# Four of sixteen weight preparation jobs of layer two placed, part by part, behind attention steps of eight later head pairs

## The chip, the cores and the metric

The kernel runs on one core of one Trainium2 chip. The metric is the device time of one execution in microseconds (us), the median of several runs. Matrix products run on TensorE (PE, with its weight loads as PEld), elementwise work on VectorE (DVE) and ScalarE (ACT), reductions over partitions on GpSimd (POOL); SyncE (SP) issues nearly all DMA transfers.

## The reference

Three stages follow one another. The first is attention with random features over 4 x 8 heads of 576 positions, head size 64, 128 features:

```python
proj = einsum('bhsd,df->bhsf', x, w_phi)
proj = proj - max(abs(proj), axis=-1, keepdims=True)
phi  = concatenate([exp(proj), exp(-proj)], axis=-1)
kv   = einsum('bhsf,bhsd->bhfd', phi(k), v);  z = sum(phi(k), axis=2)
out  = (phi(q) @ kv) / (phi(q) @ z + 1e-06)
```

Its output, as 2304 tokens of 512 values, goes through layer one, `max(0.01*h, h) @ w_out` with `h = x @ w_in` (512 to 2048 to 512), and then through layer two, `(h * sigmoid(h)) @ w_out`, with weights of its own of the same sizes. The weights of the layers come as 64-bit floats, so each must be turned into 32-bit ones on the chip.

## The kernel before

**Precision.** Each operand of the layers is held as a high part and a low part (`split`, L683: ACT copies the high part, DVE subtracts it, L262), and a product is three matmuls. Layer one takes the tokens in five tiles (`tiles1`: 462, 462, 460, 460, 460) and the hidden size in 16 chunks. For each (tile, chunk), `h_mm` (L821) does 12 matmuls (L830) into a bank of the set "a", `h_g` applies the leaky ReLU on ACT (tile g, L836), `h_high` and `h_low` split the result (gh on ACT, L841; gl on DVE), and `y_mm` (L851) does 12 matmuls (L861) of them with `wo[c]`, one chunk late. From the second tile on, `wo[c]` is loaded back from memory by `load_wo` (L783): 512 KB on SP, from the ring "wo1", and from the ring "wo2" once attention is over.

**Attention** runs in 16 pairs of heads. The first eight are done in an order written out by hand; the later eight (8 to 15) go one after the other between some 187 and 385 us, in the shadow of layer one, each over three chunks of a tile. The list `seq` holds their steps with a due time each, from the offsets in `OFF1` (L606): lv, lq (loads), sp (split), pq, pk, pkt (projections), eq0 and eq1 (exponentials of q, by halves), kv, num0 and num1 (numerators and denominators, L571 and L572 on ACT: tiles d and x), fin0 and fin1 (multiply x by the reciprocal of the denominator, and split it into the xh and xl of a token tile, L407). `run_att` (L630) takes the steps that are due from `seq` and writes them; the main loop calls it twice per (tile, chunk). The order on each engine is then made by a scheduler, which keeps data dependences and what `behind` asks for: `behind(spot, f, ...)` runs f and holds its instructions, on each engine, behind the one that `spot` names for that engine.

**Weight preparation of layer two** is `prep_w7` (L700), a generator of five parts per job, 2 x 8 jobs. Part one loads 512 KB of raw weights on SP (`load64`, ring "raw") and narrows them to fa: ACT takes the absolute value t (L657) and scales the other word to r (L658), DVE does four operations (L664, 665, 666, 670). Part two does the same for fb. Part three forms two pairs of sums on DVE (L717 to L720). Part four puts fa and half of fb: `put` splits into a tile wst (ACT L684, DVE L262) and SP stores it in `w7s` (L713). Part five puts the sums. `jobs_of` (L1060) gives each part a cost of 1.8, the last 1.6.

Before the change, `run_jobs` (L1075) takes parts only once `seq` is empty, with 3.4 credits for each of the remaining (tile, chunk) steps, so the first job begins near 360 us. What is left of the sixteen jobs after layer one is done in the first groups of layer two, up to a given job before each.

Of the kernel before, what the change touches and what calls it, by code (L numbers as in the profile page):

```python
# [9 lines left out]
F32R = mybir.dt.float32r  # L10
# [111 lines left out]
def tile_linear_attention_ffn_ffn(ctx: ExitStack, tc: tile.TileContext, q, k, v, w_phi, w_in1, w_out1, w_in2, w_out2, out):  # L122


    nc = tc.nc
# [9 lines left out]
    WOB = 3  # L135
    RAWB = 3
# [7 lines left out]
    wp = ctx.enter_context(tc.tile_pool(name="wp", bufs=1))  # L144
# [27 lines left out]
    pins = {mybir.EngineType.PE: [], mybir.EngineType.Activation: [], mybir.EngineType.DVE: [], mybir.EngineType.SP: []}  # L172

    def in_order(f, i, ts):

        seen = len(nc.cur_bb.bb.instructions)
        f(i)
        m, was = 0, None
        for ins in nc.cur_bb.bb.instructions[seen:]:
            if ins.engine in pins:  # L180
                m, was = min(m + (was not in (None, ins.engine)), len(ts) - 1), ins.engine
                pins[ins.engine].append((ts[m], ins))
# [11 lines left out]
    def behind(first, f, *a):  # L194

        seen = len(nc.cur_bb.bb.instructions)
        r = f(*a)
        nosync = mybir.DependencyInfo(mybir.DependencyClass.NoSync, mybir.DependencyReason.DATA)
        for ins in nc.cur_bb.bb.instructions[seen:]:
            if ins.engine in first:  # L200
                tc.add_manual_dep(ins, first[ins.engine].name, nosync, reason="order")
        return r
# [128 lines left out]
    def part(i, a):  # L331

        return ((0, 256), (256, 320))[a] if full(i) else ((0, HALF), (HALF, HALF))[a]
# [273 lines left out]
    seq = [(t, i, n_) for n_, ts in ORDER.items() for i, t in enumerate(ts)]  # L607
# [9 lines left out]
    seq.sort()  # L617
    seq.reverse()

    def missing(t):  # L620
        a0, n0 = tiles1[t]
        for _, i, n_ in seq:
            if n_[:3] in ("fin", "ffx"):
                c0, w = part(i, int(n_[3]))
                lo = i // HP * S + c0
                if lo < a0 + n0 and lo + w > a0:
                    return True
        return False

    def run_att(until, tile_=None):  # L630
        while seq and (seq[-1][0] < until or (tile_ is not None and missing(tile_))):
            if AB[0] is ABUFS0 and seq[-1][2] in OFF1:
                att0_ctx.close()
                att_pool[0] = att_ctx.enter_context(tc.tile_pool(name="att1", bufs=1))
                AB[0] = ABUFS1
            t, i, n_ = seq.pop()
            PRO[0] = t < RING
            if n_ in head or (i, n_) in EARLY:
                in_order({**fns, **head}[n_], i, EARLY.get((i, n_), (t,)))
            else:  # L640
                behind(low if n_[:3] == "fin" else {}, fns[n_], i)


    x2 = drp.tile([KD, 128, NT], F32, name="x2")
# [2 lines left out]
    def load64(src):  # L647

        raw = wp.tile([128, 512, 2], U32, tag="raw", bufs=RAWB, name="raw")
        nc.sync.dma_start(raw, src)  # L650
        return raw
# [27 lines left out]
    def narrow64(raw):  # L679

        return narrow_dve(*narrow_act(raw))

    def split(f, h, l):  # L683
        nc.scalar.activation(h, f, AF.Copy)  # L684
        sub(l, f, h)
# [8 lines left out]
    def words(w, c):  # L694
        return w.bitcast(U32)[c].rearrange("p (f t) -> p f t", t=2)

    def load_wo64(w, c):
        return load64(w.bitcast(U32)[c * 128 : (c + 1) * 128, :].rearrange("p (f t) -> p f t", t=2))

    def prep_w7(m_, p):  # L700

        ld = (lambda c: load64(words(w_in2, c))) if m_ == 0 else (lambda c: load_wo64(w_out2, c))
        fa = narrow64(ld(2 * p))
        yield
        fb = narrow64(ld(2 * p + 1))
        yield
        lo, hi = slice(0, 256), slice(256, 512)

        def put(i, x):
            m = x.shape[1] // 256  # L710
            o = wp.tile([128, m, 2, 256], F32R, tag="wo1", bufs=WOB, name="wst")
            split(x.rearrange("p (m f) -> p m f", f=256), o[:, :, 0], o[:, :, 1])
            nc.sync.dma_start(w7s[m_, p, :, i : i + m], o.bitcast(F32))  # L713

        s12 = wp.tile([128, 512], F32, tag="t64", bufs=2, name="s12")
        s34 = wp.tile([128, 512], F32, tag="t64", bufs=2, name="s34")
        nc.vector.tensor_tensor(s12[:, lo], fb[:, lo], fb[:, hi], op=ALU.add)  # L717
        nc.vector.tensor_tensor(s12[:, hi], s12[:, lo], fa[:, lo], op=ALU.subtract)
        nc.vector.tensor_tensor(s34[:, lo], fa[:, lo], fb[:, lo], op=ALU.subtract)
        nc.vector.tensor_tensor(s34[:, hi], fa[:, hi], s12[:, hi], op=ALU.subtract)  # L720
        yield
        put(0, fa)
        put(2, fb[:, hi])
        yield
        put(3, s12)
        put(5, s34)
# [328 lines left out]
    wake()  # L1055
    split_consts()
    run_att(END - 1e-3)
    pin()

    def jobs_of(m, p):  # L1060
        for _ in prep_w7(m, p):
            half[0] = True
            yield NP * m + p, 1.8
        half[0] = False
        yield NP * m + p, 1.6

    jobs = (x for m in range(2) for p in range(NP) for x in jobs_of(m, p))
# [14 lines left out]
    for s, (t, c) in enumerate((t, c) for t in range(len(tiles1)) for c in range(NC)):  # L1082
        if s < len(SLOTS):
            continue
        run_att(T0 + pace(s + 0.5) + 0.21, t if c == 0 else None)
        emit_h(t, c)
        run_att(T0 + pace(s + 1) + 0.21)
        if prev is not None:
            emit_y(*prev)
        prev = (t, c)  # L1090
        if not seq and s1p[0] is None:
            att_ctx.close()
            s1p[0] = ctx.enter_context(tc.tile_pool(name="s1", bufs=1))
        if s1p[0] is not None:
            run_jobs(RATE[0])
            if t == len(tiles1) - 1:
                if c in (2, 5):
                    settle()
                    next(x_first)
                if c >= 9:  # L1100
                    next(h_first)
# [103 lines left out]
```

## Time and profile before

| | us |
|---|---|
| median of 3 runs | 939.24 (939.15 to 939.47) |
| the profiled execution | 938.98 |
| its span, first to last instruction | 937.2 |
| PE busy | 931.2 (99%) |
| weight loads of PE busy | 882.5 (94%) |
| DVE busy | 646.3 (69%) |
| ACT busy | 598.2 (64%) |
| POOL busy | 77.7 (8%) |

A busy share is of the whole span. The profile divides the span into stages only where windows are asked for, and idle time of an engine is put down to what ended it. An engine's operations overlap a little at their ends, so two neighbours may show less time from start to start than the first one's length.

### The profile page before, as it was taken

To read this page: it belongs to the slowest core of one execution; us is meant where nothing else is said; L and a number is where in the kernel's file an instruction comes from. 1 tells how busy PE (TensorE), PEld (TensorE's weight loads), DVE (VectorE), ACT (ScalarE), POOL (GpSimd) and SP (SyncE) were. 2 spreads that over 40 slices of the span, in tenths; PEclk is the share of its full clock that TensorE was granted. 3 is DMA by queue.
4 is the path that set the end of the run, shared out by engine and by line. 5 is a ranking of instruction groups with operands and counts; after the bars stand their busy time and mean duration, and the time that the engine had idled before them with its cause. 6 is when DMAs were issued, how large, how long until landed. Compare 5 with 4: busy or idle time off the path is not lost.

```text
span 937.2 us, 15718 instructions
## 1 busy us (share of the span) xinstructions
PE 931.2 (99%) x5430; PEld 882.5 (94%) x5430; DVE 646.3 (69%) x1280; ACT 598.2 (64%) x1224; POOL 77.7 (8%) x50
## 2 busy tenths in 40 slices
PE   8999999999999999999999999999999999999998
PEld 7999989999999999988888999999999999999998
DVE  6889999966656655587777577879553685534853
ACT  6888787877777775565554456666644556444553
POOL 4442000111111110000000000000000000000000
PEclk9999999999999999999999999999999999999999
DMA  6854474573333434699999987998898778986785
GB/s 228 283 181 165 147 247 150 175 232 106 116 122 96 129 102 122 216 391 352 350 323 359 377 306 288 351 350 298 271 303 274 239 245 270 307 277 219 250 268 164
DMA packets 101759, 226.13 MB, mean 241 GB/s; under 512 B 15024, under 2 KB 25264, under 8 KB 101680
## 3 DMA queue, kind: packets, MB, share of 16 engines
q1 hardware_dynamic: 100432, 220.14, 69.2%
q0 software_dynamic: 960, 4.72, 1.3%
q8 instruction: 44, 0.72, 0.3%
q14 instruction: 35, 0.29, 0.1%
q10 hardware_dynamic: 288, 0.26, 0.1%
HBM read 177.82 MB, written 47.22 MB: 240 GB/s over the span
## 4 chain that ended last, share of the span: by engine, by line
PE 97%; ACT 1%; DVE 1%; DMA 1%; POOL 0%; SPq 0%; issue 0%; DVEq 0%; ACTq 0%
PE ps_a L830 21%; PE ps_y L861 21%; PE ps_y L1019 19%; PE ps_a L942 10%; PE ps_y L942 9%; PE ps_a L385 5%; PE ps_a L568 3%; PE ps_a L516 2%; PE ps_y L385 1%; PE ps_y L516 1%; PE ps_a L380 1%; DMA qr<-in_q_dram 1%; PE ps_a L345 0%; PE ps_a L346 0%; PE ps_a L315 0%; PE ps_a L314 0%
## 5 line engine op out<-in xcount | busy, mean ns | idle before, releaser
L830 PE MATMUL ps_a<-xh,wi 128*128 128x460 f32 (+1 forms) x640 | 195.2, 372 | 0.0
L1019 PE MATMUL ps_y<-gt,ws 128*128 128x384 f32 x1008 | 177.2, 336 | 0.0
L1019 PEld LDWEIGHTS ps_y<-gt,ws 128*128 128x128 f32 x1008 | 176.5, 188 | 0.0
L861 PE MATMUL ps_y<-gh,wo 128*128 128x460 f32 (+1 forms) x640 | 148.5, 371 | 0.0
L830 PEld LDWEIGHTS ps_a<-xh,wi 128*128 128x128 f32 x640 | 120.3, 188 | 12.9
L861 PEld LDWEIGHTS ps_y<-gh,wo 128*128 128x128 f32 x640 | 119.5, 188 | 13.0
L830 PE MATMUL ps_a<-xl,wi 128*128 128x460 f32 (+1 forms) x320 | 118.7, 371 | 0.0
L942 PE MATMUL ps_a<-xs,ws 128*128 128x384 f32 x546 | 104.6, 338 | 0.0
L942 PEld LDWEIGHTS ps_a<-xs,ws 128*128 128x128 f32 x546 | 96.8, 188 | 0.4
L684 ACT ACTIVATE gt<-g 128x384 fp32r<-128x384 f32 x120 | 63.0, 525 | 51.7 <-PE ps_y L1019 50.1
L262 DVE TENSOR_TENSOR gt<-g,gt 128x384 fp32r<-128x384 f32 x120 | 66.1, 555 | 32.2 <-ACT gt L684 31.5
L942 PE MATMUL ps_y<-xs,ws 128*128 128x384 f32 x462 | 88.2, 338 | 0.0
L861 PE MATMUL ps_y<-gl,wo 128*128 128x460 f32 (+1 forms) x320 | 82.1, 373 | 0.0
L942 PEld LDWEIGHTS ps_y<-xs,ws 128*128 128x128 f32 x462 | 81.8, 188 | 0.0
L262 DVE TENSOR_TENSOR gl<-g,gh 128x460 fp32r<-128x460 f32 (+1 forms) x80 | 50.9, 636 | 34.4 <-ACT gh L841 20.0
L836 ACT ACTIVATE g<-ps_a 128x460 f32<-128x460 f32 (+1 forms) x80 | 44.2, 552 | 40.7 <-PE ps_a L830 40.1
L861 PEld LDWEIGHTS ps_y<-gl,wo 128*128 128x128 f32 x320 | 60.1, 188 | 6.9
L830 PEld LDWEIGHTS ps_a<-xl,wi 128*128 128x128 f32 x320 | 60.3, 188 | 6.0
L841 ACT ACTIVATE gh<-g 128x460 fp32r<-128x460 f32 (+1 forms) x80 | 46.9, 586 | 18.8 <-PE ps_y L861 17.0
L350 POOL PARTITION_ALL_REDUCE m<-p x16 | 35.4, 2216 | 228.8 <-ACT p L348 183.7
L934 ACT ACTIVATE g<-g 128x384 f32<-128x384 f32 x72 | 37.4, 520 | 20.2 <-DVE g L917 20.1
L385 PE MATMUL ps_a<-va,ke 128*128 128x128 f32 x384 | 46.9, 275 | 0.0
(170 smaller groups left out, 1505.5 us busy)
## 6 DMA issues: line engine op xcount, KB each, us to landing
ws<-w7s SPq DMA_DIRECT2D x336, 256.0 KB, 4.2
wo<-wos SPq DMA_DIRECT2D x64, 512.0 KB, 5.0
w7s<-wst SPq DMA_DIRECT2D x48, 512.0 KB, 5.9
raw<-in_moe_w_out_dram SPq DMA_DIRECT2D x32, 512.0 KB, 5.7
rawi<-in_moe_w_in_dram SPq DMA_DIRECT2D x16, 512.0 KB, 6.1
wos<-wo SPq DMA_DIRECT2D x16, 512.0 KB, 2.9
raw<-in_moe_w_in_dram SPq DMA_DIRECT2D x16, 512.0 KB, 6.2
va<-in_v_dram SPq DMA_DIRECT2D x16, 325.0 KB, 5.3
```

The lines of the kernel that those rows point to most:

```text
L262: return nc.vector.tensor_tensor(out_, x, h.bitcast(F32), op=ALU.subtract)
L350: nc.gpsimd.partition_all_reduce(m, p, 128, bass_isa.ReduceOp.absmax)
L385: nc.tensor.matmul(pv[:, s, j], ke[:, g, s, :], vf[:, w : w + NKV], start=False, stop=(j == 1 and c == 3), skip_group_check=True)
L516: nc.tensor.matmul(pb[:, w : w + NNUM], e[:, s, cs], KV[:, s, j], start=(s == 0), stop=(s == 1))
L684: nc.scalar.activation(h, f, AF.Copy)
L830: nc.tensor.matmul(ph, a[:, kk, :], b_[:, kk, :], start=(m == 0), stop=(m == 3 * KD - 1))
L836: nc.scalar.activation(g, G[t, c]["ph"], AF.Prelu, alpha=0.01)
L841: low[mybir.EngineType.Activation] = nc.scalar.activation(gh, G[t, c]["g"], AF.Copy).ins
L861: nc.tensor.matmul(Y[t][d][:, 0:n], a[:, ds_], b_, start=(c == 0 and m == 0), stop=(c == NC - 1 and m == 1), skip_group_check=True)
L934: nc.scalar.activation(g[j], x, AF.Silu)
L942: nc.tensor.matmul(bank[b_], w[:, a, kk], x[:, c, kk], start=(first and m == 0), stop=(m == 5), skip_group_check=True)
L1019: nc.tensor.matmul(bank[b_][db], w[:, a, db], t[:, c], start=(first and p == 0 and m == 0), stop=(p == NP - 1 and m == 2), skip_group_chec ...
```

## The change

`run_att` gets a table `SPARE` of twenty steps of the pairs 8 to 15. After it has written such a step, it runs one part of the preparation, and holds it, on each engine, behind the last instruction that the step itself wrote there (for eq1: behind the first instruction that the step wrote, on that one's engine). After four jobs nothing more is taken this way. The other twelve jobs are taken as before by `run_jobs`. And `put` takes its tile from the ring "raw" (3 tiles, that of the raw loads) as long as `seq` isn't empty, else from "wo1" as before. The conditional with `if False` always gives the table's number, 1. Lines move by 10 or 11: L657 is L667 after, L684 L694, L713 L724, L788 L799, L830 L841, L836 L847, L841 L852, L877 L888.

```diff
--- before.py
+++ after.py
@@ -617,6 +617,9 @@
     seq.sort()
     seq.reverse()
 
+    early, EARLY_JOBS = [0], 4
+    SPARE = {(8, 'fin0'): 1, (8, 'fin1'): 1, (9, 'eq1'): 1, (9, 'fin0'): 1, (9, 'fin1'): 1, (10, 'fin0'): 1, (10, 'fin1'): 1, (11, 'eq1'): 1, (11, 'fin0'): 1, (11, 'fin1'): 1, (12, 'fin0'): 1, (12, 'fin1'): 1, (13, 'eq1'): 1, (13, 'fin0'): 1, (13, 'fin1'): 1, (14, 'fin0'): 1, (14, 'fin1'): 1, (15, 'eq1'): 1, (15, 'fin0'): 1, (15, 'fin1'): 1}
+
     def missing(t):
         a0, n0 = tiles1[t]
         for _, i, n_ in seq:
@@ -638,7 +641,14 @@
             if n_ in head or (i, n_) in EARLY:
                 in_order({**fns, **head}[n_], i, EARLY.get((i, n_), (t,)))
             else:
+                seen = len(nc.cur_bb.bb.instructions)
                 behind(low if n_[:3] == "fin" else {}, fns[n_], i)
+                if (i, n_) in SPARE and early[0] < EARLY_JOBS:
+                    own = [x for x in nc.cur_bb.bb.instructions[seen:] if x.engine in pins]
+                    step = (EARLY_JOBS * 5 - 1 if False else SPARE[i, n_])
+                    spot = {x.engine: x for x in (own if n_ != "eq1" else own[:1])}
+                    for _ in range(step):
+                        early[0] += behind(spot, next, jobs)[1] == 1.6
 
 
     x2 = drp.tile([KD, 128, NT], F32, name="x2")
@@ -708,7 +718,8 @@
 
         def put(i, x):
             m = x.shape[1] // 256
-            o = wp.tile([128, m, 2, 256], F32R, tag="wo1", bufs=WOB, name="wst")
+            tag, n = ("wo1", WOB) if not seq else ("raw", RAWB)
+            o = wp.tile([128, m, 2, 256], F32R, tag=tag, bufs=n, name="wst")
             split(x.rearrange("p (m f) -> p m f", f=256), o[:, :, 0], o[:, :, 1])
             nc.sync.dma_start(w7s[m_, p, :, i : i + m], o.bitcast(F32))
```

Where the parts come to stand shows on ACT and SP. The first place is ACT in pair 12, at the end of the second token tile (312 to 319 us in the profile of before). xh are the pieces of x for the coming tile, KVH the split state of the pair, e and m exponentials of q. Before:

```order
L398 ACTIVATE KVH<-ps_a 128x2x64 x3
L407 ACTIVATE xh<-x 128x172
L836 ACTIVATE g<-ps_a 128x462
L841 ACTIVATE gh<-g 128x462
L407 ACTIVATE xh<-x 128x288
L367 ACTIVATE e<-m 128x576
L271 ACTIVATE krh<-kr 128x512
L367 ACTIVATE m<-m 128x576
L571 ACTIVATE d<-ps_a 1x288
L572 ACTIVATE x<-ps_a 64x288
L299 ACTIVATE ke<-ke 128x4x128
```

After:

```order
L407 ACTIVATE xh<-x 128x172
L667 ACTIVATE t_3632<-raw 128x512
L668 ACTIVATE r_3633<-raw 128x512
L847 ACTIVATE g<-ps_a 128x462
L852 ACTIVATE gh<-g 128x462
L367 ACTIVATE e<-m 128x576
L271 ACTIVATE krh<-kr 128x512
L367 ACTIVATE m<-m 128x576
L407 ACTIVATE xh<-x 128x288
L667 ACTIVATE t_3732<-raw 128x512
L668 ACTIVATE r_3733<-raw 128x512
L571 ACTIVATE d<-ps_a 1x288
```

Two |t| and two r (t_ and r_ with a number, L667 and L668) stand behind the two xh, ahead of the first g and of the first d.

A little further on the same engine (320 to 327 us), before:

```order
L877 ACTIVATE o<-ps_y 128x462
L348 ACTIVATE p<-ps_a 128x288 x2
L277 ACTIVATE qs<-qr 64x576 x2
L836 ACTIVATE g<-ps_a 128x460
L281 ACTIVATE kth<-kt 128x128
L877 ACTIVATE o<-ps_y 128x462
L841 ACTIVATE gh<-g 128x460
L571 ACTIVATE d<-ps_a 1x288
L572 ACTIVATE x<-ps_a 64x288
```

After:

```order
L888 ACTIVATE o<-ps_y 128x462
L348 ACTIVATE p<-ps_a 128x288 x2
L277 ACTIVATE qs<-qr 64x576 x2
L300 ACTIVATE ke<-ke 128x4x128
L847 ACTIVATE g<-ps_a 128x460
L281 ACTIVATE kth<-kt 128x128
L571 ACTIVATE d<-ps_a 1x288
L572 ACTIVATE x<-ps_a 64x288
L888 ACTIVATE o<-ps_y 128x462
L571 ACTIVATE d<-ps_a 1x288
L572 ACTIVATE x<-ps_a 64x288
L852 ACTIVATE gh<-g 128x460
```

gh, which followed the second o, now stands behind two d, two x and that o as well.

The third place is SP where the ring "wo2" is opened (379 to 390 us). The wo tiles are numbered by the program. Before:

```order
L581 DMA d<-rec 64x288 x2
L713 DMA w7s<-wst 128x1024
L713 DMA w7s<-wst 128x512
L788 DMA wo_4394<-wos 128x1024
L788 DMA wo_4441<-wos 128x1024
L788 DMA wo_4492<-wos 128x1024
```

After:

```order
L581 DMA d<-rec 64x288 x2
L660 DMA raw<-in_moe_w_in_dram 128x1024
L724 DMA w7s<-wst 128x1024
L724 DMA w7s<-wst 128x512
L660 DMA raw<-in_moe_w_in_dram 128x1024 x2
L799 DMA wo_4562<-wos 128x1024
L799 DMA wo_4609<-wos 128x1024
```

One raw load now stands ahead of the two stores and two more between them and the first loads of wo.

## Rows read from the trace of the kernel before

**Rows 1.** The page: busy us (share) xinstructions, and the chain that ended last, by engine.

```profile
PE 931.2 (99%) x5430; PEld 882.5 (94%) x5430; DVE 646.3 (69%) x1280; ACT 598.2 (64%) x1224; POOL 77.7 (8%) x50
...
PE 97%; ACT 1%; DVE 1%; DMA 1%; POOL 0%; SPq 0%; issue 0%; DVEq 0%; ACTq 0%
```

**Rows 2.** Chain of waits: its longest link (start us, us, what).

```profile
875.01 58.81 PE ps_y L1019 x336
```

**Rows 3.** Windows: stretch, then PE, PEld, DVE, ACT, POOL busy, clock, DMA share, GB/s.

```profile
187.00:256.00 69.00, 69.00 (x421) 64.52 (x420) 44.32 (x83) 54.31 (x115) 12.07 (x6) 1.00 0.51 157
...
256.00:325.00 69.00, 69.00 (x429) 64.74 (x428) 43.79 (x86) 51.41 (x112) 12.85 (x6) 1.00 0.37 113
```

**Rows 4.** Groups by line and form on ACT: busy us, mean ns, idle before.

```profile
L657 ACT ACTIVATE t<-raw 128x512 f32<-128x512 f32 x32 | 21.3, 665 | 5.2 <-DVE wst L262 3.9 <-DVE r L670 1.3
...
L658 ACT ACTIVATE r<-raw 128x512 uint32<-128x512 uint32 x32 | 21.0, 666 | 4.9 <-DVE wst L262 4.4 <-DMA raw<-in_moe_w_in_dram 0.4 <-DVE s L720 0.2
...
L684 ACT ACTIVATE wst<-s 128x512 fp32r<-128x512 f32 x32 | 19.9, 623 | 3.3 <-DMA w7s<-wst 2.9 <-DVE s L718 0.3
...
L684 ACT ACTIVATE wst<-r 128x256 fp32r<-128x256 f32 x16 | 6.7, 416 | 20.0 <-DVE r L670 14.6 <-DMA w7s<-wst 4.3 <-issue 1.1
```

**Rows 5.** The same view on DVE: subtraction of a put.

```profile
L262 DVE TENSOR_TENSOR wst<-s,wst 128x512 fp32r<-128x512 f32 x32 | 22.0, 689 | 22.3 <-ACT wst L684 22.2
```

**Rows 6.** Timeline of ACT, 229 to 250 us: start us, us, operation [idle before <-releaser].

```profile
233.60 0.28 ACT L398 ACTIVATE KVH<-ps_a 128x128 fp32r<-128x128 f32 x1 [1.39 <-PE ps_a L385]
...
239.12 0.45 ACT L407 ACTIVATE xh<-x 128x288 fp32r<-128x288 f32 x1 [1.07 <-DVE x L588]
...
247.99 0.56 ACT L836 ACTIVATE g<-ps_a 128x462 f32<-128x462 f32 x1
```

**Rows 7.** Timeline of PE, 241 to 250 us.

```profile
249.60 0.38 PE L830 MATMUL ps_a<-xh,wi 128*128 128x462 f32 x1
```

**Rows 8.** Timeline of ACT, 311 to 329 us (pair 12).

```profile
312.10 0.35 ACT L407 ACTIVATE xh<-x 128x172 fp32r<-128x172 f32 x1 [0.59 <-PE ps_a L830]
...
314.59 0.45 ACT L407 ACTIVATE xh<-x 128x288 fp32r<-128x288 f32 x1 [1.08 <-DVE x L588]
...
315.26 0.69 ACT L367 ACTIVATE e<-m 128x576 f32<-128x576 f32 x1 [0.22 <-DVE m L360]
...
323.62 0.56 ACT L836 ACTIVATE g<-ps_a 128x460 f32<-128x460 f32 x1
...
325.00 0.56 ACT L877 ACTIVATE o<-ps_y 128x462 f32<-128x462 f32 x1 [0.48 <-DMA x<-o]
...
325.45 0.58 ACT L841 ACTIVATE gh<-g 128x460 fp32r<-128x460 f32 x1
...
326.06 0.40 ACT L571 ACTIVATE d<-ps_a 1x288 f32<-1x288 f32 x1
```

**Rows 9.** Timeline of PE, 318 to 331 us.

```profile
324.78 0.37 PE L830 MATMUL ps_a<-xh,wi 128*128 128x460 f32 x1
...
327.27 1.84 PE L861 MATMUL ps_y<-gh,wo 128*128 128x460 f32 x8
```

**Rows 10.** Timeline of SP's queue, 379 to 394 us.

```profile
381.03 4.65 SPq L713 DMA_DIRECT2D w7s<-wst  x2
...
385.90 1.28 SPq L788 DMA_DIRECT2D wo<-wos  x3
```

**Rows 11.** One tile: wo, 379 to 400 us, its loads from issue to landing.

```profile
DMA to landing us min/median/max: 4.3/6.4/8.1
```

**Rows 12.** Timeline of PE, 383 to 393 us.

```profile
391.02 1.84 PE L861 MATMUL ps_y<-gh,wo 128*128 128x460 f32 x8
```

**Rows 13.** Timeline of ACT, 379 to 393 us.

```profile
384.45 0.42 ACT L684 ACTIVATE wst<-r 128x256 fp32r<-128x256 f32 x1 [3.69 <-DMA w7s<-wst]
```

**Rows 14.** Timeline of all engines, 247 to 248 us.

```profile
247.10 2.14 POOL L350 PARTITION_ALL_REDUCE m<-p  x1 [10.03 <-DVE ql L262]
...
247.28 1.73 DVE L262 TENSOR_TENSOR qs<-qr,qs 64x576 fp32r<-64x576 f32 x1 [0.34 <-ACT qs L277]
```

## The prediction, made before the run

> **What bounds the kernel now.** I read the page's busy shares and clock first, then the chain of waits, the windows by stage, and the timelines of the places that the change reaches. PE is busy 99% of the span, and the chain that ended last is 97% PE [rows 1]. Its longest link is 336 matmuls back to back in 58.81 us, 0.175 us each [rows 2]. In the stretch that the change fills, PE is busy for the whole of both windows, 187 to 256 and 256 to 325 us, and its granted clock is 1.00 (the 2.4 GHz level) [rows 3]. ACT is busy 54.31 of 69.00 us (79%) and DVE 44.32 of 69.00 (64%) in the first of these windows. So nothing that is moved away from ACT, DVE or SP can give time back. Only a new wait of PE can change the time. What has to be asked of each part is whether it makes ACT, DVE or a load late by more than PE's margin there.
>
> **What is removed, added, moved.** PE, ACT, DVE and SP keep their instruction counts but for how rows are grouped; nothing new is computed. Twenty parts, four jobs of weight preparation, go from the stretch after some 360 us into the eight later pairs, one job per two pairs: the first pair gets the two narrowing parts, behind fin0 and fin1, the second the sums behind eq1 and the two puts behind fin0 and fin1. The bookkeeping (early[0], spot) is run by the host when the program is built and costs nothing on the chip.
>
> Work moved per job. ACT has two |t| at 0.665, two r at 0.666, three 512-wide wst at 0.623 and one of 256 at 0.416 us [rows 4]: 1.33 + 1.33 + 1.87 + 0.42 = 4.95 us. DVE has sixteen operations (eight of narrowing, four sums, four subtractions) of which none takes over the 0.689 us of a 512-wide subtraction [rows 5], so at most 11.0 us. A pair lasts some 25 us; half a job is 2.5 us of ACT and at most 5.5 us of DVE. ACT's idle share of 21% is 5.3 us per pair and DVE's 36% is 9 us, so both have room on average. SP has two loads of 512 KB and four stores per job more in the pairs; the DMA engines are half busy there (0.51, then 0.37 [rows 3]), so bandwidth covers them. In SP's queue a store waits for its subtraction (0.689 us), and behind it are the small moves (d, e, rec) of the pair's halves: those come up to 0.7 us late each, which I take as 0, since their user is fin, whose x PE reads with the next tile. POOL's queue gets nothing. What would uncover either is a place where the room isn't when the part comes.
>
> **Ordinary pairs.** A part with one |t| and one r is 1.33 us. ACT's waits there are 1.39 us before KVH at 233.60 and 1.07 us before xh at 239.12 [rows 6]: the part behind fin0 fits the first, the one behind fin1 overhangs the second by 0.26. Walking the new order by hand with these durations, g comes 0.3 to 0.6 us late. PE's margin to it: g ends at 247.99 + 0.56 = 248.55 [rows 6], and PE starts the next L830 matmul, which takes that bank, at 249.60 [rows 7], so 1.05 us. The stall is 0; bounds 0 and, if a second overhang adds, 0.2 per pair. I take 0 because 0.6 is under 1.05, and put 0.2 in all for the pairs that I did not walk.
>
> **Place A, pair 12 (312 to 329 us).** Here fin0 cannot run early: its xh of 172 columns waits for PE to finish tile 1 (0.59 us, before 312.10 [rows 8]), and both parts of the pair fall between there and 318. After 315.26 ACT has no wait until the 0.48 before o at 325.00 [rows 8]. So 2 x 1.33 = 2.66 us, less the idle time before it that they can use (1.08 and 0.22, the rows of 314.59 and 315.26), leave 1.36 us of lateness; engines start the next operation a little before the last one's end shows, and the hand walk gives 1.4. g, before at 323.62 to 324.18, then ends near 325.55. PE wants that bank at 324.78 [rows 9]: stall 0.8 us. The order also puts gh, which ended at 326.03 before, behind kth, two pairs of d and x and one o: 0.3 + 4 x 0.4 + 0.56, and 0.58 for gh itself [rows 8], 3.0 us after 325.55, or 328.45 with the overlaps taken off; PE's y matmuls want it at 327.27 + 0.8 = 328.07 [rows 9]: 0.4 more. Sum **1.2 us**, bounds 0 (if lateness is under g's margin of 324.78 - 324.18 = 0.60) and 2.0 (if nothing of the idle time can be used: 2.66 - 0.60). I take 1.2, nearest to the row of g.
>
> **Place B, the switch at 380 to 393 us.** Before, SP issues two stores of w7s from 381.03 and, after the second's ring slot came free, three loads of wo at 385.90 [rows 10]. They land 4.3 us or more after issue [rows 11], so at 390.2, and PE uses the first at 391.02 [rows 12]: a margin of 0.8. After, a raw load precedes the stores, and two more raw loads precede wo. Their slots are those of the two stores (the put now takes the raw ring), so SP waits there for each store to land, and the wo loads wait behind SP. The first store was seen to release its slot at 384.45, 3.4 us after issue [rows 13]; the second lands some 1 to 3 us later. So wo is issued at 386.0 to 387.4, say 387.0, as the third load in a row. At 4.3 (the least) to 6.4 us (the median [rows 11]) it lands at 391.3 to 393.4. The order gives PE three more matmuls ahead (0.6 us), so it is wanted at 391.65: stall 0 to 1.75, middle **0.9 us**. Here SP's own queue is moved past: nothing but these loads is behind it until the next w7s.
>
> The twelve jobs that remain end earlier (105.6 credits at 3.4 a step, 31 steps in place of 41; a job costs 4 x 1.8 + 1.6 = 8.8). What they leave idle on ACT and DVE lies beside a PE that has no wait there either: the window of layer two's last products is a row of 336 matmuls at one spacing [rows 2]. Worth nothing.
>
> **Sum.** 0.2 + 1.2 + 0.9 = 2.3 us. The profiled execution took 938.98 us (937.2 of span and 1.8 around it), 0.26 under the median of the three runs. 938.98 + 2.3 = 941.3 against that one execution; against the median, 939.24 + 2.3 = **941.6**. Bounds 0 to 4.0 us. A change of 0.2% is 1.9 us, about what can be told from none.
>
> **The port of DVE and POOL.** During the reduction of 2.14 us on POOL at 247.10, a subtraction of DVE with two operands in memory (576 wide) took 1.73 us from 247.28 [rows 14], where the 512-wide one of preparation, on twice the partitions, takes 0.689 [rows 5]. So the reduction's company cost it about 1.0 us. The moved DVE operations include such two-operand ones, so a collision may add about as much on DVE, which the holes that DVE has take up unless it is late already; I take 0. The Trainium skill, "SBUF — State Buffer", section "SBUF: two separate sides", calls it an exclusive lock, held for a whole instruction, on which the loser fully blocks; by that rule the sum would grow by the reduction's rest each time, and the row is in line with a lengthened operation without showing who held what.
>
> **Rivals.**
> (1) The holes cover all: in place A the scheduled order leaves g inside its 0.60, in place B wo lands at the least latency. Then 939.24 + 0.1 = 939.3. For it: the margins of about 1 us in the ordinary pairs and the low DMA share. Against: ACT without a wait from 316 to 324 us. It ends on the other side (not slower).
> (2) The switch costs more: the wait is on two landings in sequence, and ACT's r, which reads the raw load, stands ahead of gh. Should the second store take 8.1 us, the slowest of the loads seen [rows 11], from some 382, SP is let go at 390 and not at 387, and 3 us come on top: 941.6 + 3.0 = 944.6; half of that, 1.5 us, gives 943.1. It decides when that store takes over 5 us.
> (3) DVE becomes late beside POOL's reductions: half of the 1.0 us, past the margins, in half of the eight pairs: 4 x 0.5 = 2.0 us on top, 943.6. It decides once a moved operation and the reduction meet ahead of a subtraction that PE waits for. For: the row of 1.73 us. Against: the DVE's idle third.
> (4) PE runs faster, because its matmuls overlap and come down to the time of its weight loads: 882.5 us [rows 1] in place of 937.2, so 939.24 - 54.7 = 884.5 at the most. Against it, the spacing is a constant 0.21 us in one layer and 0.175 in the other [rows 2, 9], and the change touches neither. The Trainium skill, "Perfetto Trace Analysis", section "Identifying the Most-Contended Engine", says that matmul busy time is no good measure of how near TensorE is to its limit, and that the busy share of weight loads is; by that rule there is room, by the rows of spacing there is none.
> (5) The change doesn't do what it says: the scheduler places the parts after the pairs. The orders quoted show otherwise, so I give it nothing apart from (1).
>
> **How the numbers follow.** Forecast as worked out (0.5 to 4.0 us slower): 0.52. Rival 1: 0.26; rival 2: 0.12; rival 3: 0.06; rival 4: 0.03; 0.01 for none of them. The forecast's own range is 940.3 to 942.9. About a quarter of its weight (0.13) lies under 941.1, the bound of "slower". Same: 0.26 + 0.13 = 0.39. Slower: 0.39 + 0.12 + 0.06 = 0.57, with the rest 0.58. Faster 0.03. The range that holds 8 in 10 goes from rival 1 (939.0 with its scatter) to 943.4, leaving out the upper half of rivals 2 and 3 and all of rival 4, some 0.15.
>
> **What would show it.** Right: PE waits of 0.5 to 1.5 us on ACT g or gh near 325 us, and one on a wo load near 391 us, with everything else on PE unchanged at 0.21 us per matmul; the window of 187 to 325 us without PE idle time. Wrong: no PE idle time over 0.1 us in either place (rival 1), DVE operations of over 1 us beside POOL's reductions and PE waits in each pair (rival 3), or PE idle time after 400 us, where I see no reason for any.

## The result, and the profile after

The changed kernel takes 948.01 us (median of 4 runs, 944.86 to 948.70) against 939.22 us (939.15 to 939.47): a ratio of 1.0085, 95% interval 1.0066 to 1.0105. That is 8.8 us slower, well outside the range of 939.0 to 943.4. The direction was right, the size was not. The profile shown is of the run of 948.70 us, whose span is 946.9 us, 9.7 longer than before.

The page of the changed kernel, busy time by engine and the chain that ended last, to set beside [rows 1]:

```profile
PE 935.9 (99%) x5430; PEld 884.3 (93%) x5430; DVE 645.2 (68%) x1280; ACT 596.8 (63%) x1224; POOL 77.9 (8%) x50
...
PE 81%; issue 7%; ACT 5%; DMA 3%; DVE 3%; POOL 0%; SPq 0%; ACTq 0%; DVEq 0%; POOLq 0%
```

The instruction counts are as before, and so is the busy time of DVE and ACT (0.2% less): no work was added. The share of PE in the chain fell from 97 to 81%, and ACT, DMA and DVE rose from 1% each to 5, 3 and 3%. The 7% of "issue" is no loss of its own: nearly all of it is one link in layer two, during which PE was busy throughout.

```profile
577.30 56.46 issue
```

So PE waits where it had not. The waits of PE from 180 us on (engine, line, waited for: us in all, times, longest):

```profile
PE ps_a L841 <- ACT x L572: 1.9, 2, 1.3
PE ps_y L872 <- ACT gh L852: 1.8, 1, 1.8
PE ps_y L953 <- DVE g L928: 0.9, 1, 0.9
PE ps_a L841 <- ACT g L847: 0.7, 1, 0.7
```

The kernel before had no wait of PE there at all. The windows that hold them (columns as in [rows 3]: stretch; PE, PEld, DVE, ACT, POOL busy; granted clock; DMA share; GB/s):

```profile
212.00:237.00 25.00, 23.72 (x147) 21.92 (x146) 21.03 (x41) 21.04 (x46) 3.96 (x2) 1.00 0.42 107
262.00:287.00 25.00, 24.43 (x150) 22.68 (x149) 20.80 (x43) 20.17 (x44) 4.61 (x2) 1.00 0.34 95
312.00:337.00 25.00, 24.21 (x148) 22.22 (x148) 20.41 (x43) 21.77 (x48) 4.57 (x2) 1.00 0.39 123
...
391.00:396.00 5.00, 4.51 (x14) 3.94 (x15) 3.73 (x8) 3.69 (x8) 0.00 (x0) 0.66 0.77 255
```

Three of the four narrowing pairs (8, 10 and 12) lose PE time, then the switch near 390 us, where layer one goes on without attention and the granted clock is also 0.66; the wait on DVE's g is in layer two, at 649 us. A place is named here by the pair whose fin0 and fin1 the parts follow; the KVH, KVL, d and x that stand beside them are steps of the pair after it. The idle time in the windows is less than the whole loss, since the first matmul after a wait also takes longer (0.48 us and not 0.37 at 222.17 below). Taking matmul by matmul how much later each ends after its predecessor than that kind normally does, the profile gives 1.8 us at 221 to 223, 0.8 at 273, 1.3 at 329 to 332, 2.1 + 1.5 + 0.3 at 390 to 400 and 1.5 in layer two: 9.3 of the 9.7 us.

**At 221 us**, the wait of 1.3 us on x. ACT of the changed kernel (timeline, 207 to 224 us):

```profile
212.02 0.28 ACT L398 ACTIVATE KVH<-ps_a 128x128 fp32r<-128x128 f32 x1 [0.56 <-DVE KVL L262]
213.72 0.28 ACT L398 ACTIVATE KVH<-ps_a 128x128 fp32r<-128x128 f32 x1 [1.42 <-DVE KVL L262]
214.36 0.28 ACT L398 ACTIVATE KVH<-ps_a 128x128 fp32r<-128x128 f32 x1 [0.36 <-DVE KVL L262]
...
216.78 0.45 ACT L407 ACTIVATE xh<-x 128x288 fp32r<-128x288 f32 x1 [1.07 <-DVE x L588]
217.13 0.67 ACT L667 ACTIVATE t<-raw 128x512 f32<-128x512 f32 x1
217.70 0.66 ACT L668 ACTIVATE r<-raw 128x512 uint32<-128x512 uint32 x1
...
221.71 0.41 ACT L572 ACTIVATE x<-ps_a 64x288 f32<-64x288 f32 x1
```

and DVE and POOL in the same stretch:

```profile
208.45 0.19 DVE L577 RECIPROCAL e<-e 96x6 f32<-96x6 f32 x1 [1.76 <-DMA e<-d]
208.56 0.45 DVE L588 TENSOR_TENSOR x<-x,d 128x288 f32<-128x288 f32 x1
...
211.91 1.58 DVE L680 CUSTOM_DVE_ANT_0 r<-t,r 128x1024 uint16<-128x1024 uint16 x1
213.41 0.28 DVE L262 TENSOR_TENSOR KVL<-ps_a,KVH 128x128 fp32r<-128x128 f32 x1
...
211.56 2.23 POOL L350 PARTITION_ALL_REDUCE m<-p  x1 [11.90 <-ACT p L348]
```

ACT is not full here: it waits 0.56 and 1.42 us for DVE's KVL. DVE does the narrowing of the part behind fin0 between the KVL subtractions, and one operation of it, L680, takes 1.58 us beside POOL's reduction. In the kernel before, with PE 0.31 us earlier (an L346 matmul at 219.81 and at 220.12), the same three operations of ACT stood so:

```profile
210.96 0.28 ACT L398 ACTIVATE KVH<-ps_a 128x128 fp32r<-128x128 f32 x1 [0.36 <-DVE KVL L262]
...
214.07 0.45 ACT L407 ACTIVATE xh<-x 128x288 fp32r<-128x288 f32 x1 [1.08 <-DVE x L588]
...
218.65 0.41 ACT L572 ACTIVATE x<-ps_a 64x288 f32<-64x288 f32 x1
```

Against PE, the last KVH is 3.1 us late (214.36 - 210.96 - 0.31), xh 2.4 and x 2.75. PE's matmul that takes x's bank is late by 222.17 - 220.20 - 0.31 = 1.7 (its rows, of after and of before):

```profile
222.17 0.48 PE L841 MATMUL ps_a<-xh,wi 128*128 128x462 f32 x1 [1.28 <-ACT x L572]
```

```profile
220.20 0.37 PE L830 MATMUL ps_a<-xh,wi 128*128 128x462 f32 x1
```

so its margin (220.20 - 218.65 - 0.41 = 1.1 us in the rows of before) was used up and 1.7 went on top.

The part also began late, because the step that it follows did. fin0's multiply (L588) starts at 208.56 here, behind a reciprocal that waited 1.76 us for a small move of SP. In the kernel before it starts at

```profile
206.78 0.46 DVE L588 TENSOR_TENSOR x<-x,d 128x288 f32<-128x288 f32 x1 [0.45 <-DMA d<-rec]
```

so it is 1.5 us late against PE. In all seven kernels of this document with one narrowing part ahead of these KVL, the last KVL starts 6.1 us after that multiply, which is 0.3 to 1.5 us late; in the kernel with the part behind kv (below) the multiply is 1.1 us late as well, and no KVL is. So the loss here needs the part's place and varies with the moves ahead of it.

**At 329 us**, place A of the prediction (PE of the changed kernel):

```profile
328.66 0.48 PE L841 MATMUL ps_a<-xh,wi 128*128 128x460 f32 x1 [0.73 <-ACT g L847]
```

The forecast there was 0.8 us on g and 0.4 on gh; measured matmul by matmul, 1.0 and 0.3.

**At the switch** (SP's queue, ACT and PE, 384 to 400 us):

```profile
384.21 1.12 SPq L581 DMA_DIRECT2D d<-rec  x2
385.38 0.58 SPq L660 DMA_DIRECT2D raw<-in_moe_w_in_dram  x1
386.06 0.85 SPq L724 DMA_DIRECT2D w7s<-wst  x2
391.52 0.93 SPq L660 DMA_DIRECT2D raw<-in_moe_w_in_dram  x2
393.58 0.80 SPq L799 DMA_DIRECT2D wo<-wos  x2
```

```profile
390.31 0.66 ACT L668 ACTIVATE r<-raw 128x512 uint32<-128x512 uint32 x1 [5.86 <-DMA raw<-in_moe_w_in_dram]
390.87 0.57 ACT L852 ACTIVATE gh<-g 128x460 fp32r<-128x460 f32 x1
```

```profile
391.49 2.76 PE L872 MATMUL ps_y<-gh,wo 128*128 128x460 f32 x8 [1.82 <-ACT gh L852]
394.06 1.73 PE L872 MATMUL ps_y<-gl,wo 128*128 128x460 f32 x4
```

The raw load of the next job comes behind the last d and rec moves of pair 15 in SP's queue and lands near 390.2. ACT's r, which needs it, stands in front of gh, and ACT sits for 5.86 us. PE waits 1.82 us, and soon after its matmuls come 0.38 us apart and not 0.21: eight took 2.76 us, four 1.73, where the same stretch before shows 1.84 for eight [rows 12]. The window above gives 0.66 of the full clock for 391 to 396, so part of the stretch was at the lower of the two levels, 1.2 GHz, after PE had stood still; that alone costs 1.5 us. In the run of 944.86 us the mean clock was 1.000, in the other three 0.998; by that figure, the shortest of the four had no such stretch.

### The profile page after: what moved, and what is told of

Its sections match the earlier page's. It is cut to its first block, busy times and chain, and to the rows that moved or that the text cites. A ratio compares the mean times of both kernels' runs of the same rounds, so it can differ in the third digit from the quotient of the medians.

```text
span 946.9 us, 15703 instructions
## 1 busy us (share of the span) xinstructions
PE 935.9 (99%) x5430; PEld 884.3 (93%) x5430; DVE 645.2 (68%) x1280; ACT 596.8 (63%) x1224; POOL 77.9 (8%) x50
## 4 chain that ended last, share of the span: by engine, by line
PE 81%; issue 7%; ACT 5%; DMA 3%; DVE 3%; POOL 0%; SPq 0%; ACTq 0%; DVEq 0%; POOLq 0%
PE ps_y L1030 19%; PE ps_a L841 18%; PE ps_y L872 17%; PE ps_y L953 6%; PE ps_a L953 6%; PE ps_a L385 4%; PE ps_a L516 2%; PE ps_a L568 2%; PE ps_y L385 1%; DMA wo<-wos 1%; PE ps_y L516 1%; DMA e<-d 1%; ACT x L572 1%; DMA b<-x 1%; PE ps_a L380 1%
## 5 line engine op out<-in xcount | busy, mean ns | idle before, releaser
L841 PE MATMUL ps_a<-xh,wi 128*128 128x460 f32 (+1 forms) x640 | 195.3, 373 | 2.6 <-ACT x L572 1.9
L841 PEld LDWEIGHTS ps_a<-xh,wi 128*128 128x128 f32 x640 | 120.3, 188 | 16.3 <-ACT x L572 2.3
L841 PE MATMUL ps_a<-xl,wi 128*128 128x460 f32 (+1 forms) x320 | 118.8, 371 | 0.0
L694 ACT ACTIVATE gt<-g 128x384 fp32r<-128x384 f32 x120 | 62.9, 525 | 51.0 <-PE ps_y L1030 50.2
L847 ACT ACTIVATE g<-ps_a 128x460 f32<-128x460 f32 (+1 forms) x80 | 44.1, 551 | 37.9 <-PE ps_a L841 37.4
L841 PEld LDWEIGHTS ps_a<-xl,wi 128*128 128x128 f32 x320 | 60.4, 189 | 6.1
L852 ACT ACTIVATE gh<-g 128x460 fp32r<-128x460 f32 (+1 forms) x80 | 46.8, 585 | 19.6 <-PE ps_y L872 18.4
```

Of the source, the lines that this page charges most:

```text
L841: nc.tensor.matmul(ph, a[:, kk, :], b_[:, kk, :], start=(m == 0), stop=(m == 3 * KD - 1))
L847: nc.scalar.activation(g, G[t, c]["ph"], AF.Prelu, alpha=0.01)
L852: low[mybir.EngineType.Activation] = nc.scalar.activation(gh, G[t, c]["g"], AF.Copy).ins
```

## The experiments

The theory was that the loss is a sum of separate places: DVE's narrowing in the KVL chain at pairs 8 and 10, ACT at pair 12, and r ahead of gh at the switch. The rivals: ACT is overloaded in general; the loss goes with the number of jobs; or the switch is late because of the wo loads (the prediction's view).

**Fewer jobs.** Two early jobs, and, with a 3 in that place, three:

```diff
-    early, EARLY_JOBS = [0], 4
+    early, EARLY_JOBS = [0], 2
```

> Two jobs in place of four (pairs 8 to 11), the ring change kept. If each loss belongs to the job that stands there, only the two PE waits at pairs 8 and 10 are left (1.8 and 0.8 us in the changed kernel's profile): 941.8 us, or 943.3 if the 1.5 us lost in layer two come with any early job; no wait near 390 us. If the loss comes from the twelve or more jobs being cut from the later stretch as a whole (layer two's rhythm), 945 or more.

> Three jobs in place of four (pairs 8 to 13). By the theory of one loss per place: 939.2 + 1.8 + 0.8 + 1.3 = 943.1 us (944.6 with layer two's 1.5), no wait on gh near 390 us and no half-clock matmuls there, since the raw loads of the next job come before the switch again. Rival (the switch is late because layer one's end has the wo loads in a row, whatever the job): a wait of 1 us or more near 390 us stays.

Measured: 941.96 us with two (ratio 1.0029, 1.0016 to 1.0041) and 944.08 with three (1.0055, 1.0040 to 1.0070), both beside 939.11. With three jobs PE's waits are the first and the last row of the change's own list, with the same figures, and no other. There is none at the switch: it belongs to the fourth job. In the two profiles the places add up as the theory says (1.3 and 1.1 us at pairs 8 and 10 with two jobs, and 0.6 in layer two; 1.6, 0.9 and 1.3 at pairs 8, 10 and 12 with three), but the median with three is 1.0 us over the 943.1 expected without a loss in layer two.

**The narrowing part behind kv** of the next pair in place of fin0, in the four pairs:

```diff
-    SPARE = {(8, 'fin0'): 1, (8, 'fin1'): 1, ...
+    SPARE = {(9, 'kv'): 1, (8, 'fin1'): 1, ...
```

> All four jobs, but the part that stood behind fin0 stands behind the kv step of the pair after it, so behind the last KVL on DVE and the last KVH on ACT. If DVE's narrowing ahead of the KVL subtractions makes KVH, g and x late, the waits at pairs 8 and 10 go (2.6 us) and most of that at pair 12: 944.5 to 945.5 us with the switch's loss left. If ACT's 1.33 us of added work makes x late, nothing is won: 947 to 949 us.

Measured: 944.53 us (942.81 to 944.75). PE's waits in the profile (its fastest run):

```profile
PE ps_a L841 <- ACT g L847: 1.3, 1, 1.3
PE ps_y L872 <- DMA wo<-wos: 1.0, 1, 1.0
```

The waits on x at pairs 8 and 10 are gone, as expected. What is lost at pair 12 grew from 1.3 to 1.9 us, on g and gh. So the place in the KVL chain is needed for the first, and not for the second. At the switch the raw load left SP at 379.83 us in this run, r ran at 385.20, and gh was in time; then the late wo loads showed, for 1.0 us. The first of them landed at 394.29 (388.49 + 5.8), and PE began 0.35 us after that:

```profile
394.64 1.91 PE L872 MATMUL ps_y<-gh,wo 128*128 128x460 f32 x8 [1.04 <-DMA wo<-wos]
```

So the prediction's wait at the switch exists where the raw load is not later still.

**The fourth job's puts in the ring wo1:**

```diff
-            tag, n = ("wo1", WOB) if not seq else ("raw", RAWB)
+            tag, n = ("wo1", WOB) if not seq or early[0] > 2 else ("raw", RAWB)
```

> All four jobs, but the fourth job's puts take their tiles from the ring wo1 as before the change, so that the next job's raw load needn't wait for stores. If the switch's loss (2.1 us on gh, 1.5 of half clock, 0.3 behind it) is ACT's r waiting for that raw load ahead of gh: 948.0 - 3.9 = 944.1 us, and gh near 390 us is no longer waited for. If it is the three loads of wo in a row or the number of jobs: 947 to 949 us.

Measured: 943.14 us (943.04 to 944.54). The raw loads now go out at 364 and 372 us, before pair 15's last moves (SP's queue of this kernel), and r finds its data (ACT):

```profile
364.30 0.50 SPq L660 DMA_DIRECT2D raw<-in_moe_w_in_dram  x1
```

```profile
382.22 1.22 ACT L668 ACTIVATE r<-raw 128x512 uint32<-128x512 uint32 x2 [0.45 <-DVE wst L262]
```

PE has no wait at the switch. So the new ring is what makes the switch late: a raw load of the fifth job is queued behind tiles of the fourth job's puts. The edit won 4.9 us, and the switch accounts for 3.9 of them. The rest is in places that it does not touch: in this profile pair 8 lost 1.0 us and pair 10 nothing, so these two vary by over 1 us between runs.

**Both edits together**, the two diffs above in one kernel:

> Both edits together: the fin0 part behind kv, and the fourth job's puts in the ring wo1. If the losses are separate mechanisms they add: only pair 12 (1.9 us in the profile with the part behind kv) and 0.3 to 0.7 us of layer two are left, 941.3 to 941.8 us, with no wait at pairs 8 and 10 nor near 390 us. If the losses only move (a wait saved in one place comes back in another), 943 us or more.

Measured: 942.27 us (941.30 to 943.28), 0.5 above the range given. The profile, of a run of 941.74, has one wait of PE left, 1.3 us on g at pair 12: the other places are free at the same time. The gains of the two edits do not add up in the medians (3.5 and 4.9 us alone, 5.7 together), since the kernel with the part behind kv lost less at the switch already, 1.3 us and not 3.9 in its profile. The runs scatter more than those of the kernel before.

**Without pair 12.** The same, with three jobs in the pairs 8 to 11, 14 and 15 (the entries of 12 and 13 are taken out of `SPARE`); the third is now the one whose puts are in wo1:

```diff
-    early, EARLY_JOBS = [0], 4
+    early, EARLY_JOBS = [0], 3
...
-            tag, n = ("wo1", WOB) if not seq else ("raw", RAWB)
+            tag, n = ("wo1", WOB) if not seq or early[0] > 1 else ("raw", RAWB)
```

> Three jobs in the pairs 8 to 11, 14 and 15, none in 12 and 13, with both edits (part behind kv, last job's puts in wo1). If PE has nothing to win and every loss has been named, this is level with the kernel before: 939.1 to 939.9 us, never under 938.5. If earlier preparation is worth something once the waits are gone, 938 or less; if the losses scale with the number of jobs, 941 us or more.

Measured: 939.76 us (10 runs, 939.12 to 940.51) against 939.19, ratio 1.0007 (0.9998 to 1.0016): level. PE's only wait from 180 us on:

```profile
PE ps_y L953 <- DVE g L928: 0.3, 1, 0.3
```

Three jobs done early, with the waits in layer one taken away, win nothing. What the profile still loses, 0.9 us, is in layer two.

**ACT or DVE at pair 8.** The part behind fin0 split: its ACT operations stay there, its DVE operations go behind kv; the fourth job's puts are in wo1:

```diff
-        fa = narrow64(ld(2 * p))
+        fa = narrow_act(ld(2 * p))
+        if seq:
+            yield 0.0
+        fa = narrow_dve(*fa)
...
+    SPARE = {(8, 'fin0'): 1, (9, 'kv'): 1, (8, 'fin1'): 1, ...
```

> The part that stood behind fin0 is split: its two ACT operations stay behind fin0, its four DVE operations go behind kv of the next pair; the fourth job's puts are in wo1. If DVE's operations ahead of KVL cause the waits at pairs 8 and 10: no wait there, some 941 to 942 us. If ACT's t and r ahead of KVH cause them: the wait of 0.8 us or more at pair 8 stays and the time is that of the kernel with the wo1 edit alone, 943.1 us.

Measured: 942.21 us (941.84 to 942.44), 0.2 above the range given and 0.9 under the kernel with the wo1 edit alone, with no wait on x (a wait of 0.4 us on gh at 397 us is new). The last of pair 8's four KVL is at 211.32 us, where the changed kernel has it at 214.67 and the kernel before at 211.27. ACT's two operations ahead of KVH do no harm to it; DVE's four do.

**r behind gh**, with SP's order and the rings of the change:

```diff
-            at_p[0], cost = behind(gate, next, jobs, (2 * NC, credit[0]))
+            at_p[0], cost = behind({**gate, **low}, next, jobs, (2 * NC, credit[0]))
```

> All of the change, but a part taken by run_jobs stands, on ACT and DVE, also behind the gh and gl written last, so that at the switch r comes behind gh and no longer ahead of it. SP's order and the rings are as in the change. If r waiting for its raw load ahead of gh is the switch's loss: the gh wait (1.8 us), the half clock (1.5) behind it go, and what is left there is at most 1 to 1.3 us for the late load of wo: 944.5 to 946 us. If the late loads alone are the loss: 947 to 949 us.

Measured: 944.69 us (944.56 to 945.44), 3.3 under the change and in the range given. One wait of 1.25 us is left at the switch, one chunk later (ACT, PE and SP of this kernel, and its wo loads of 384 to 402 us):

```profile
393.95 0.57 ACT L852 ACTIVATE gh<-g 128x460 fp32r<-128x460 f32 x1
...
396.30 0.59 ACT L852 ACTIVATE gh<-g 128x460 fp32r<-128x460 f32 x1
```

```profile
396.88 1.93 PE L872 MATMUL ps_y<-gh,wo 128*128 128x460 f32 x8 [1.25 <-ACT gh L852]
```

```profile
390.33 0.80 SPq L799 DMA_DIRECT2D wo<-wos  x2
...
DMA to landing us min/median/max: 6.2/8.5/10.3
```

PE's row names gh, but gh does not fit. The gh that these matmuls read ended at 394.52, over 2 us before they began; the next one ended at 396.89, just after. They also need the first of the two wo loads, which landed 6.2 us after its issue, at 396.53, and PE begins 0.35 us after that, as behind wo in the kernel with the part behind kv. So this wait is on wo. With r out of the way, the prediction's late wo load is what is left of the switch. In the change it was hidden: PE, held up by gh, came to that load only 0.3 us too early. After the shorter wait the clock stays at the higher level.

**One job, and one job with both narrowing parts ahead of KVL.** `EARLY_JOBS` is 1 in both; the second also has:

```diff
-    SPARE = {(8, 'fin0'): 1, (8, 'fin1'): 1, (9, 'eq1'): 1, ...
+    SPARE = {(8, 'fin0'): 2, (9, 'eq1'): 1, ...
```

> One early job alone (pairs 8 and 9). One part of narrowing ahead of KVL in pair 8: a PE wait there of 1.3 to 1.8 us, as in the kernels with two and three jobs, and no other: 940.5 to 941.2 us. If losses of the pairs come from the loads or the stores of the jobs rather than from DVE's order, the wait at pair 8 is under 0.5 and the time 939.2 to 939.8.

> One early job, but both its narrowing parts stand behind fin0 of pair 8, so that eight DVE operations and not four are spread ahead of the four KVL. If DVE ahead of KVL sets the loss, the wait at pair 8 grows by the second part's operations, 0.43 + 0.45 + 0.69 + 0.69 = 2.3 us less small overlaps: 942.4 to 943.5 us. If ACT's two more operations alone count, by 0.7 to 1.1 us less: 941.3 to 942.2. If the wait has another cause, as with one part: 940.5 to 941.2.

Measured: 940.43 us (939.63 to 940.96) with one job, 0.1 under the range given, and 940.78 (939.66 to 941.66) with both parts ahead: a miss for the theory, which had 942.4 or more. In the profile of the second (its fastest run), KVH waits longer for DVE than in the change, yet PE's wait is short (ACT, then PE):

```profile
213.06 0.28 ACT L398 ACTIVATE KVH<-ps_a 128x128 fp32r<-128x128 f32 x1 [1.82 <-DVE KVL L262]
...
216.24 0.45 ACT L407 ACTIVATE xh<-x 128x288 fp32r<-128x288 f32 x1 [1.63 <-DVE x L588]
...
219.67 0.41 ACT L572 ACTIVATE x<-ps_a 64x288 f32<-64x288 f32 x1
```

```profile
220.13 0.48 PE L841 MATMUL ps_a<-xh,wi 128*128 128x462 f32 x1
```

From xh to x it takes 3.4 us here, 4.9 in the change: no t and r stand between them, and ke stands behind x. Against PE, which stood 0.3 us earlier than in the kernel before, xh is 2.5 us late (2.4 in the change), but x only 1.3, 0.2 over the margin. So in this run the late KVL alone cost little, and it takes the second part, behind fin1, to make the change's loss. This is the fastest of ten runs: the median is no better than with one job, and where the slower runs lose is not shown. An operation of DVE was slow beside POOL again, L675, with one operand in memory (0.43 us elsewhere):

```profile
211.30 1.52 DVE L675 TENSOR_SCALAR t<-t 128x512 uint32<-128x512 uint32 x1
```

**The second part elsewhere**, in all four narrowing pairs behind num0 of the next pair (fourth job's puts in wo1), and in a second kernel the first part behind kv as well:

```diff
-    SPARE = {(8, 'fin0'): 1, (8, 'fin1'): 1, ...
+    SPARE = {(8, 'fin0'): 1, (9, 'num0'): 1, ...
```

> All four jobs, the fourth's puts in wo1, and the second narrowing part no longer behind fin1 but behind the num0 step of the pair after it, so behind d and x on ACT. If it takes both parts together to use up the margin of x (DVE's ahead of KVL makes KVH and xh 2.4 us late, ACT's t and r behind xh add 1.1), the wait at pair 8 shrinks to 0.5 us or less, and that of g at pair 12 loses up to 1.1: 940.5 to 941.7 us. If DVE's part ahead of KVL is enough alone: the wait at pair 8 stays at 1 us or more, 942.3 to 943.4.

> As that, with the first narrowing part behind kv too: no part ahead of KVL and none between xh and x. If place alone makes the loss, all four jobs then cost nothing in the pairs: 939.2 to 940.3 us (up to 1 us of layer two's waits), as with three jobs that leave out pair 12. If a job in pair 12 costs ACT time whatever its place: 941 to 942. Nothing under 938.5 by any of them, as PE has no wait to win back.

Measured: 948.95 us (947.05 to 953.21) and 946.29 (943.21 to 947.58), both far above what was expected. At pair 8 the first did what the theory says: KVL is late (1.9 us against PE, and 3.1 in the change) and an operation of DVE takes 1.58 us beside POOL again, but PE starts on time,

```profile
219.92 0.37 PE L841 MATMUL ps_a<-xh,wi 128*128 128x462 f32 x1
```

with no wait at 273 or 329 us either. From the last KVL to the end of x it takes 6.7 us here, and 7.5 in the change with t and r between them. The loss turns up in the pairs after (the two largest of PE's waits from 180 us on, first kernel):

```profile
PE ps_y L872 <- DMA wo<-wos: 1.0, 2, 0.5
PE ps_a L841 <- ACT x L572: 1.0, 2, 0.5
...
```

There the sums and the puts now follow close behind a narrowing part that begins later, which may be the reason; no run tested it. So a part's place has to be right for the pair after it too; no free place for it was found with num0.

## Why the prediction was wrong

By the profile the terms of the sum were 2.6 us for the ordinary pairs, 1.3 for place A and 3.9 for place B, forecast as 0.2, 1.2 and 0.9, and 1.5 in layer two, forecast as nothing. (939.24 + 2.3 is 941.5 and not 941.6, and the forecast's own range is narrower than its 0.5 to 4.0 us; neither made the miss.)

**What bounds the kernel: right.** PE had nothing to win, and only new waits moved the time. The kernel without pair 12 shows it: with no wait left in layer one, three early jobs gain nothing.

**Ordinary pairs: the step that failed first.** It put 0.2 us on them. They cost 1.8 + 0.8 = 2.6 us in the profile; one job alone costs 1.5 (940.43 against 938.97). The walk fitted the part behind fin0 into a hole of ACT of 1.39 us [rows 6], and costed its DVE operations by the pair's average idle share ("both have room on average"). That hole stands behind fin0 of pair 9, which gets puts; behind fin0 of pair 8 the kernel before has 0.95 us:

```profile
208.76 0.28 ACT L398 ACTIVATE KVH<-ps_a 128x128 fp32r<-128x128 f32 x1 [0.95 <-PE ps_a L385]
```

And only the first KVH waits for PE. Each later one waits for DVE's KVL (0.36 us at 210.96), so this is the time in which DVE has to be free. The four operations take 2.2 us there at their usual lengths, and 3.1 in the change. The split part showed that DVE's place is what matters. That it needs the second part as well, t and r between xh and x, to pass PE's margin by so much, rests on two profiles: without it x was 1.3 and 0.8 us late, with it 2.75 (2.4 at xh and 0.35 more up to x), against 1.1. The prediction looked at PE's margin to g, 1.05 us [rows 6, 7], and let the x of the same pair go by. It also took the late small moves as 0, "since their user is fin, whose x PE reads with the next tile"; but the part hangs behind fin0, so fin0's lateness of up to 1.5 us went on to KVL.

**Place A: right.** Forecast 1.2 us on g and then gh, measured 1.3, by the mechanism that was named. With the first part behind kv it was 1.9.

**Place B: the wait that was forecast stood behind a longer one, 0.9 for 3.9.** The forecast had wo as the late load. Where r is out of the way, PE does wait for wo: 1.25 us with r behind gh, 1.0 with the part behind kv, inside the 0 to 1.75 that were given. In the change the wait was on gh, behind r and its raw load. That was a half-sentence in rival 2 ("ACT's r, which reads the raw load, stands ahead of gh"), at 0.12, and that rival's condition came true: SP went on 5.5 us after it had issued the stores (386.06 to 391.52), and wo left at 393.58, not at 387.0. The order quoted ahead of the prediction already had the raw load behind pair 15's d. The step also left out 1.5 us of half clock, which no row of before could show, since PE never stood still there.

**DVE beside POOL (rival 3): took part.** The operation of L680 took 1.58 us behind fin0 of pair 8 in each of the seven kernels that kept one narrowing part there, against 0.69 behind fin0 of pair 10 in the change, where it began before the reduction (263.18 against 263.43 us). That is 0.9 us of pair 8's lateness. The Trainium skill's "SBUF — State Buffer", section "SBUF: two separate sides", has the one that comes second block until the other is done, if the DVE operation has two inputs in SBUF, as this one has; that the first to start went unhindered in pair 10 agrees. How long it was held does not: with its usual length taken off, it was let go at 211.91 + 1.58 - 0.69 = 212.80, 1.2 us into a reduction of 2.23, and L675 in the kernel with both parts ahead at 211.30 + 1.52 - 0.43 = 212.39, also 1.2 us into its reduction (from 211.16), by the profile's times, which are rough for POOL. The prediction saw such a row [rows 14] and took 0 because DVE had idle time, the same mistake as above.

**Layer two: 0 for 1.5 us.** The loss of 0.3 us at 571 came in the profiles of all kernels with a job in the pairs 14 and 15 and in no other; the one of 1.2 at 650 (0.9 of it a wait on DVE's g, L928) came, smaller, in some other kernels and not in the rest. No run was made to settle why; that part is open.

## What to carry to other kernels

An idle stretch of an engine is free only if the engine that it waits for is free too: put the moved work on both timelines, operation by operation, and follow each engine's in-order queue to the next thing that PE needs. Margins are used up by sums: two parts that each fit can fail together. Where a wait is put down to an instruction that ended long before it, or after it, look for the other operand: at the switch it was a load. And where a moved step changes the tiles that share a ring, look at what comes next out of that ring, and what stands behind the instruction that waits for it.

## What was not expected of the hardware

After a wait of 1.82 us in a stretch that had been busy throughout, PE's matmuls ran 0.38 us apart for some three microseconds (granted clock 0.66 over 391 to 396 us), and then at 0.21 again; after the waits of 1.28 us at 221 us (clock 1.00 in that window) and 1.25 us in the kernel with r behind gh they didn't. So one wait cost nearly twice its own length: 2.1 us brought 1.5 more. And a DVE operation that began during a reduction of POOL was held up for 0.9 to 1.1 us of it, while one that began just before was not.
